# Loads in order of need, two pairs of row tiles ahead of the first gradient, and low priority for a table set-up, in a combined forward and backward kernel

## The chip, the cores and the metric

The kernel runs on one core of a Trainium2 chip. The metric is the device time of one execution in microseconds (us); where a kernel ran several times, the median is given. Engines: PE is the tensor engine, VectorE is DVE in the profile's lines, ScalarE is ACT, GpSimd is POOL, SyncE (SP, its queue SPq) issues the loads. A "tile" of rows below is 128 of the 2048 rows. `L123` in a line of the profile is a line of that kernel's source, so numbers differ by a few between kernels.

## The reference, cut to what matters

```python
def _B_ref(x, W_gate, W_up, W_down):                 # the MLP branch
    gate = einsum("bsd,df->bsf", x, W_gate)
    up = einsum("bsd,df->bsf", x, W_up)
    h = gate * (gate > 0) * up
    return einsum("bsf,fd->bsd", h, W_down)

x = A_q                                              # [1, 2048, 1024] bf16, F = 3584
xn = _layernorm(x)
out = x + _A_ref(xn, ...) + _B_ref(xn, W_gate, W_up, W_down)   # _A_ref: long convolution with 4 shift taps
# wanted: out and the gradients of all inputs for a given grad_out
```

Nearly everything is matrix products of 128 x 128 by 128 x 512. The convolution branch needs tables of sines and the shift taps in transposed form; its steps are woven between the products of the MLP.

## The kernel before: the parts that the change touches

The kernel is written against a scheduler. It lists each engine's instructions in one fixed order, by priority (`pri.now()` is high and grows weaker down the program, `pri.late()` is weaker than all of those) among what its own model of time holds to be ready. On the chip each engine then follows that list.

```python
# the start of the program
b.ln_load(x, a.frm, "frm", 0)                        # rows of tile 0
first = b.weights(B_W_gate, B_W_up, B_W_down, 0)     # W_down by transposing loads
b.layer_norm(x, xn_d, a.frm, "frm", a.tmp, "tmp", a.sm)   # loads tiles 1-3, 4-7, 8-11, 12-15; norm of all
with tc.issue_after(b.ln_act.ins), tc.issue_after(b.ln_dve.ins):
    a.tables()                                       # pri.now(); ends with the taps:
    #   load sk_b; transpose on PE; copy; store
...
# one chunk of the norm, n tiles
for j in range(n): nc.scalar.activation(..., func=ACT.Copy, accum_out=...)      # ScalarE reads the tile: sum
...                                                                              # VectorE: mean
for j in range(n):
    V.tensor_scalar(out=xt[:, j, :], ..., op0=ALU.subtract)                      # VectorE
    nc.scalar.activation(..., func=ACT.Square, accum_out=...)                    # ScalarE
...                                                                              # 3 small VectorE operations
nc.scalar.activation(out=f(4), in_=f(3), func=ACT.Sqrt)                          # ScalarE
...                                                                              # 8 small VectorE operations
for j in range(n): V.tensor_scalar(..., scalar1=self.rstd[...], op0=ALU.mult)    # VectorE; then stored
...
# hidden(): for each pair of tiles (first half: 4 pairs), with 4 PSUM buffers of 512 columns
#   2 x gate (8 matmuls each) -> relu on ScalarE
#   2 x up   (8 matmuls each) -> 2 operations on VectorE, store of h
#   transposes of the next pair on PE (flip_xn) -> copy xnT on VectorE
#   2 x gradient of h (8 matmuls each) -> copy on ScalarE, product on VectorE, store
```

## Time and profile before

| what | before |
|---|---|
| time | 2040.27 us (2038.81 to 2040.48, 3 runs) |
| span of the profiled execution | 2037.0 us |
| PE busy | 1930.9 us, 95% |
| VectorE, ScalarE busy | 995.2 us (49%), 690.4 us (34%) |
| PE idle in the first 100 us | 42 us |

PE is the engine that bounds the kernel, so only time in which it waits can be won. The prediction shows the lines that say so. When reading them, keep one caution in mind: in this profile PE has 10806 matmul records against 11014 weight loads, so 208 records are missing, and idle times of about 0.2 us scattered over the span can be such gaps and no waits.

### The profile page before, as it was taken

The page shows a single profiled execution, that of the slowest core. Times are in us where ns is not written, and L with a number is a line of the kernel's source. Part 1 is how long each engine was busy: PE and PEld are TensorE (multiplying, and loading weights), DVE is VectorE, ACT ScalarE, POOL GpSimd, SP SyncE. Part 2 cuts the span into 40 slices and gives each one's busy share as a digit, 9 for nine tenths or more (in the row PEclk, how much of TensorE's full clock was granted, in tenths as well). Part 3 has the DMA queues.
Part 4 walks back from the last instruction along what each step waited for, and adds up shares of the span by engine and source line. Part 5 has one row for each costly group of instructions (what it writes and reads, how often), then busy time and mean ns, then how long its engine had stood idle before and what let it go on. Part 6 is the DMA issues. An engine that isn't in the chain of part 4 may idle for free. (4 is left out here: it accounts for less than half of the span.)

```text
span 2037.0 us, 27072 instructions
## 1 busy us (share of the span) xinstructions
PE 1930.9 (95%) x10806; PEld 914.7 (45%) x11014; DVE 995.2 (49%) x1444; ACT 690.4 (34%) x902; POOL 20.1 (1%) x46
## 2 busy tenths in 40 slices
PE   4799999999999989999899999999989999999998
PEld 2345445444444445444444544444434444444443
DVE  4848578677687677565575740000112222223332
ACT  6456366356356347474655731111000000000000
POOL 1000000000000000000000000000000000000000
PEclk9899999999999999999999999999999999999999
DMA  9764666865565674545535269332899554454551
GB/s 266 203 160 125 160 159 172 196 174 169 156 167 161 167 192 135 152 131 153 179 119 162 73 169 334 106 119 83 182 257 233 150 134 114 114 126 119 122 128 45
DMA packets 616095, 319.10 MB, mean 157 GB/s; under 512 B 450080, under 2 KB 585248, under 8 KB 615968
## 3 DMA queue, kind: packets, MB, share of 16 engines
q1 hardware_dynamic: 614688, 313.16, 58.5%
q0 software_dynamic: 1280, 4.20, 0.6%
q8 instruction: 86, 1.41, 0.3%
q14 instruction: 41, 0.34, 0.1%
HBM read 141.36 MB, written 95.44 MB: 116 GB/s over the span
## 5 line engine op out<-in xcount | busy, mean ns | idle before, releaser
L673 PE MATMUL ps_w<-ugs,xn_nat 128*128 128x512 bf16 x1746 | 395.3, 380 | 2.7 <-issue 0.5
L673 PEld LDWEIGHTS <-xn_nat 128*128 128x128 bf16 x1792 | 171.5, 98 | 202.9 <-issue 7.1
L576 PEld LDWEIGHTS <-xnT 128*128 128x128 bf16 x1792 | 169.3, 98 | 201.2 <-issue 18.7
L576 PE MATMUL ps_h<-wdT,goT 128*128 128x512 bf16 x865 | 205.7, 382 | 13.4 <-DVE ru L634 11.4
L576 PE MATMUL ps_g<-wg,xnT 128*128 128x512 bf16 x875 | 207.8, 383 | 4.2 <-DVE ru L634 2.6
L576 PE MATMUL ps_u<-wu,xnT 128*128 128x512 bf16 x870 | 205.6, 380 | 1.7 <-issue 0.5
L673 PE MATMUL ps_d<-g_nat,hs 128*128 128x512 bf16 x866 | 203.1, 380 | 4.1 <-DMA ug_d<-ru 1.4
L757 PE MATMUL ps_o<-wd,hT 128*128 128x512 bf16 x878 | 195.0, 382 | 9.8 <-DMA hT<-h_d 8.9
L790 PE MATMUL ps_x<-wgT,ggT 128*128 128x512 bf16 x878 | 197.5, 379 | 1.0
L790 PE MATMUL ps_x<-wuT,guT 128*128 128x512 bf16 x878 | 197.3, 379 | 0.9
L759 DVE TENSOR_TENSOR o<-ps_o,ya 128x512 bf16<-128x512 f32 x32 | 21.5, 687 | 270.4 <-PE ps_o L757 269.8
L711 ACT CAST wi<-ps_w 128x512 bf16<-128x512 f32 x112 | 65.4, 585 | 255.8 <-PE ps_w L673 245.0
L757 PEld LDWEIGHTS <-hT 128*128 128x128 bf16 x896 | 87.7, 98 | 116.9 <-DMA hT<-h_d 10.8
L790 PEld LDWEIGHTS <-ggT 128*128 128x128 bf16 x896 | 87.6, 98 | 105.7
L790 PEld LDWEIGHTS <-guT 128*128 128x128 bf16 x896 | 87.6, 98 | 105.7
L576 PEld LDWEIGHTS <-goT 128*128 128x128 bf16 x896 | 84.9, 98 | 111.7 <-issue 20.2
L646 ACT CAST gh<-ps_h 128x512 bf16<-128x512 f32 x112 | 65.5, 586 | 202.5 <-PE ps_h L576 120.4
L792 DVE CUSTOM_DVE_ANT_0 gx<-ps_x,gy 128x512 f32<-128x512 f32 x32 | 22.1, 691 | 226.6 <-PE ps_x L790 212.5
L673 PEld LDWEIGHTS <-hs 128*128 128x128 bf16 x896 | 82.6, 98 | 98.7 <-issue 9.1
L281 DVE STREAM_TRANSPOSE flp<-B 128x1024 f32<-128x1024 f32 x48 | 90.1, 1934 | 47.8 <-ACT B L69 47.8
L634 DVE SCALAR_TENSOR_TENSOR ru<-ru,ps_u 128x512 bf16<-128x512 bf16 x112 | 76.0, 680 | 73.8 <-PE ps_u L576 47.9
L69 ACT CAST B<-ps 128x1024 bf16<-128x1024 f32 x96 | 95.6, 1020 | 36.0 <-PE ps L65 35.8
(152 smaller groups left out, 1707.9 us busy)
## 6 DMA issues: line engine op xcount, KB each, us to landing
ug_d<-ru SPq DMA_DIRECT2D x112, 256.0 KB, 3.4
ugs<-ug_d SPq DMA_DIRECT2D x112, 256.0 KB, 4.7
wg<-in_B_W_gate_dram SPq DMA_DIRECT2D x56, 256.0 KB, 3.4
wu<-in_B_W_up_dram SPq DMA_DIRECT2D x56, 256.0 KB, 4.6
h_d<-ht SPq DMA_DIRECT2D x112, 128.0 KB, 1.7
hs<-h_d SPq DMA_DIRECT2D x56, 256.0 KB, 4.4
out_dram<-wi SPq DMA_DIRECT2D x56, 256.0 KB, 2.1
gt<-in_grad_out_dram SPq DMA_DIRECT2D x32, 256.0 KB, 3.8
```

The costliest lines, as they stand in the source:

```text
L69: self.nc.scalar.copy(out=out, in_=in_)
L281: self.nc.vector.transpose(out=df[:, c0:c0 + 32, :], in_=sf[:, c0:c0 + 32, :])
L576: self.nc.tensor.matmul(ps[:], lhsT=xT[:, kt * P:(kt + 1) * P], rhs=w(kt), start=(kt == 0), stop=(kt == self.DT - 1))
L634: nc.vector.scalar_tensor_tensor(out=ru[s][:, 1, :], in0=ru[s][:, 0, :], scalar=0.0, in1=ps[:], op0=ALU.is_gt, op1=ALU.mult)
L646: nc.scalar.copy(out=gh[:], in_=ps[:])
L673: self.nc.tensor.matmul(ps[:], lhsT=lhsT(st), rhs=rhs(st), start=(st == 0), stop=(st == self.ST - 1))
L711: nc.scalar.copy(out=wo[:, d, :], in_=ps[:])
L757: nc.tensor.matmul(ps[:], lhsT=hT[:, kt, :], rhs=self.wd[:, kt, oc], start=(kt == 0), stop=(kt == self.FT - 1))
L759: nc.vector.tensor_tensor(out=o0[:, oc], in0=ps[:], in1=ya[:, oc], op=ALU.add)
L790: nc.tensor.matmul(ps[:], lhsT=T[:, kt, :], rhs=W[:, kt, oc], start=(i == 0), stop=(i == n - 1))
L792: V.tensor_tensor_reduce(out=gx[:, oc], in0=ps[:], in1=gy[:, oc], scale=1.0, scalar=0.0, op0=ALU.add, op1=ALU.add, accum_out=m[:, ob:ob + 1])
```

## The change

The intent is to shorten the start: bring the rows in the order in which PE needs them, give PE work that needs neither W_down nor the gradient while those load, take the wait for the taps' load off PE, load the table of the square root before it is needed, and keep the sine tables from blocking VectorE. The diff, cut to its core:

```diff
 def tables(self):
-    pri.now()
+    pri.late()
 ...
-    (taps: load, transpose on PE, copy on VectorE, store)
+def load_shift(self): ...            # the load alone
+def shift_rows(self): ...            # transpose, copy on ScalarE, store: now at the start of the convolution's steps
 ...
+    one = self.per.tile([P, 1], F32, name="one")
+    self.nc.vector.memset(one[:], 1.0)
+    self.nc.scalar.activation(out=one[:], in_=one[:], func=ACT.Sqrt)
 ...
-    LN_CHUNKS = (1, 3, 4, 4, 4)
+    LN_CHUNKS = (1, 1, 2, 4, 4, 4)
 ...  hidden():
+                ahead = fb + half == 0
+                if ahead:
+                    yield from gate_up(0)
                 for sp in range(0, HS, 2):
 ...                 (loads of the gradient's tiles)
+                    if ahead:
+                        if sp + 2 < HS:
+                            yield from gate_up(sp + 2)
+                    else:
+                        yield from gate_up(sp)
+                    yield from grad(sp)
 ...  main:
-    b.ln_load(x, a.frm, "frm", 0)
-    first = b.weights(B_W_gate, B_W_up, B_W_down, 0)
+    load(0)                                               # tile 0
+    first = [b.col_block(B_W_gate, 0, "wg")]
+    load(1)                                               # tile 1
+    first.append(b.col_block(B_W_up, 0, "wu"))
+    load(2)                                               # tiles 2, 3
+    load(3)                                               # tiles 4 to 7
+    first.append(b.row_block_T(B_W_down, 0, "wdT"))
+    goT = [b.load_T(g, i, "goT") for i in range(4)]
+    load(4)                                               # tiles 8 to 11
+    a.load_shift()
+    load(5)                                               # tiles 12 to 15
```

More of the change, by code (lines that the diff above doesn't have):

```diff
@@ L200, in tables, with load_shift, shift_rows @@
             V.tensor_copy(out=self.ident32[b:b + 32, 0, :], in_=self.identA[b:b + 32, b:b + 32])
-        sk_b = con.tile([P, self.NG * 4], BF16, name="sk_b")
-        nc.sync.dma_start(out=sk_b[:].rearrange("c (g i) -> c g i", i=4),
-                          in_=self.shift_k.rearrange("(g c) i -> c g i", c=P))
-        ps = self.ps.tile([self.NG * 4, P], BF16, name="ps_sk", tag="aps")
-        nc.tensor.transpose(ps[:], sk_b[:], self.identA[:])
-        sk_t = con.tile([self.NG * 4, P], BF16, name="sk_t")
-        V.tensor_copy(out=sk_t[:], in_=ps[:])
-        nc.sync.dma_start(out=self.sk_d, in_=sk_t[:])
+    def load_shift(self):
+        self.sk_b = self.con.tile([P, self.NG * 4], BF16, name="sk_b")
+        self.nc.sync.dma_start(out=self.sk_b[:].rearrange("c (g i) -> c g i", i=4),
+                               in_=self.shift_k.rearrange("(g c) i -> c g i", c=P))
+    def shift_rows(self):
+        ps = self.ps.tile([self.NG * 4, P], BF16, name="ps_sk", tag="aps")
+        self.pri.now()
+        self.tc.keep_in_program_order(self.nc.tensor.transpose(ps[:], self.sk_b[:], self.identA[:]))
+        sk_t = self.con.tile([self.NG * 4, P], BF16, name="sk_t")
+        self.act(sk_t[:], ps[:])
+        self.store(self.sk_d, sk_t[:])
     def tview(self, ap2d, cg):
@@ L374, in steps @@
     def steps(self):
+        self.shift_rows()
         nx = self.loads_1(0)
@@ L518, in ln_load, with layer_norm @@
         self.ln_x.append(xt)
-    def layer_norm(self, x, xn_d, xpool, xtag, jpool, jtag, spool):
+    def layer_norm(self, xn_d, jpool, jtag, spool):
         nc, D, V = self.nc, self.D, self.nc.vector
@@ L523, in layer_norm @@
         st0 = 0
-        for i in range(1, 5):
-            self.ln_load(x, xpool, xtag, i)
         for i, n in enumerate(self.LN_CHUNKS):
@@ L603, in flip_xn, with hidden @@
         return xT
-    def hidden(self, first, Wg, Wu, Wd, g, xn_d, h_d, ug_d):
+    def hidden(self, first, goT, Wg, Wu, Wd, g, xn_d, h_d, ug_d):
         nc, HS = self.nc, self.ST // 2
@@ L611, in hidden @@
             xT = [self.load_T(xn_d, s0 + i, "xnT") for i in range(HS)] if half else []
-            if not half:
-                xT += [self.flip_xn(0), self.flip_xn(1)]
-            gT = []
+            gT = [] if half else goT
             for fb in range(self.FB):
@@ L618, in hidden, with gate_up @@
                 wg, wu, wd = first if fb + half == 0 else self.weights(Wg, Wu, Wd, fb)
-                for sp in range(0, HS, 2):
-                    self.pri.now()
-                    if len(gT) < HS:
-                        gT += [self.load_T(g, s0 + sp + s, "goT") for s in range(2)]
-                    ru = [self.e2_tile("ru") for _ in range(2)]
-                    for s in range(2):
+                ru = {}
+                def gate_up(sp):
+                    while len(xT) < sp + 2:
+                        xT.append(self.flip_xn(len(xT)))
+                    for s in (sp, sp + 1):
+                        ru[s] = self.e2_tile("ru")
                         ps = self.ps_tile("ps_g")
-                        self.gemm8(ps, xT[sp + s], wg)
+                        self.gemm8(ps, xT[s], wg)
                         nc.scalar.activation(out=ru[s][:, 0, :], in_=ps[:], func=ACT.Relu)
@@ L629, in hidden @@
                         self.pri.now()
-                    for s in range(2):
+                    for s in (sp, sp + 1):
                         ps = self.ps_tile("ps_u")
-                        self.gemm8(ps, xT[sp + s], wu)
+                        self.gemm8(ps, xT[s], wu)
                         ht = self.e1_tile("ht")
@@ L636, in hidden, with grad @@
                         nc.vector.tensor_tensor(out=ht[:], in0=ru[s][:, 0, :], in1=ru[s][:, 1, :], op=ALU.mult)
-                        nc.sync.dma_start(out=h_d[(s0 + sp + s) * P:(s0 + sp + s + 1) * P, cols], in_=ht[:])
+                        nc.sync.dma_start(out=h_d[(s0 + s) * P:(s0 + s + 1) * P, cols], in_=ht[:])
                         yield 1730
                         self.pri.now()
-                    if len(xT) < HS:
-                        xT += [self.flip_xn(len(xT) + s) for s in range(2)]
-                    for s in range(2):
+                def grad(sp):
+                    for s in (sp, sp + 1):
                         ps = self.ps_tile("ps_h")
-                        self.gemm8(ps, gT[sp + s], wd)
+                        self.gemm8(ps, gT[s], wd)
                         gh = self.e1_tile("gh")
@@ L648, in hidden @@
                             "p (o f) -> p o f", o=1).to_broadcast([P, 2, 512]), op=ALU.mult)
-                        nc.sync.dma_start(out=ug_d[(s0 + sp + s) * P:(s0 + sp + s + 1) * P, :, cols], in_=ru[s][:])
+                        nc.sync.dma_start(out=ug_d[(s0 + s) * P:(s0 + s + 1) * P, :, cols], in_=ru[s][:])
                         yield 1730
                         self.pri.now()
+                ahead = fb + half == 0
+                if ahead:
+                    yield from gate_up(0)
+                for sp in range(0, HS, 2):
+                    self.pri.now()
+                    while len(gT) < min(sp + 2, HS):
+                        gT.append(self.load_T(g, s0 + len(gT), "goT"))
+                    if ahead:
[4 more added lines that the diff above has]
+                    yield from grad(sp)
     def slab(self, src, fb, name):
@@ L862 @@
     pri.now()
-    b.ln_load(x, a.frm, "frm", 0)
-    first = b.weights(B_W_gate, B_W_up, B_W_down, 0)
-    b.layer_norm(x, xn_d, a.frm, "frm", a.tmp, "tmp", a.sm)
+    load = lambda i: b.ln_load(x, a.frm, "frm", i)
+    load(0)
[9 more added lines that the diff above has]
+    load(5)
+    b.layer_norm(xn_d, a.tmp, "tmp", a.sm)
     with tc.issue_after(b.ln_act.ins), tc.issue_after(b.ln_dve.ins):
@@ L869, in mlp @@
     def mlp():
-        yield 0.9, b.hidden(first, B_W_gate, B_W_up, B_W_down, g, xn_d, h_d, ug_d)
+        yield 0.9, b.hidden(first, goT, B_W_gate, B_W_up, B_W_down, g, xn_d, h_d, ug_d)
         yield 1.3, b.grad_down(g, h_d, out_9)
@@ L874 @@
     a_steps, left = a.steps(), A_START
-    for pace, phase in mlp():
-        for ns in phase:
-            left -= ns * pace
-            while a_steps is not None and left <= 0:
-                d = next(a_steps, None)
-                if d is None:
-                    a.close()
-                    a_steps = None
-                    b.open_right(B_W_down)
-                else:
-                    left += d
+    if True:
+        for pace, phase in mlp():
+            for ns in phase:
+                left -= ns * pace
+                while a_steps is not None and left <= 0:
+                    d = next(a_steps, None)
+                    if d is None:
+                        a.close()
+                        a_steps = None
+                        b.open_right(B_W_down)
+                    else:
+                        left += d
     b.close_left()
```

## The prediction

> **What bounds the kernel now.** I read the span in slices first, then busy time in stretches of 50 us, then the tensor engine's waits in the first 120 us, then the order of time there.
>
> The page's part 2, busy tenths and granted clock in 40 slices of 51 us:
>
> ```profile
> PE   4799999999999989999899999999989999999998
> ...
> PEclk9899999999999999999999999999999999999999
> ```
>
> PE is the bound (1930.9 of 2037.0 us busy), and only the first two slices are clearly low. Three stretches put a size on it; the first figure after the stretch's length is PE's busy time:
>
> ```profile
> 0.00:50.00 50.00, 20.75 (x126) 11.05 (x128) 22.53 (x83) 33.31 (x63) 9.12 (x23) 1.00 1.01 269
> 50.00:100.00 50.00, 37.16 (x185) 17.36 (x187) 45.40 (x105) 22.84 (x34) 4.79 (x9) 0.90 0.77 196
> 100.00:150.00 50.00, 49.74 (x252) 22.06 (x256) 23.46 (x33) 25.98 (x34) 0.00 (x0) 1.00 0.63 165
> ```
>
> PE is idle for 29.2 + 12.8 = 42 us of the first 100, and for 0.3 us of the next 50. The other 64 us of idle time lie later (scattered waits up to 1250 us, 9 us around 1500 us, the last stores), where the diff changes nothing. In the same first 50 us the DMA share is 1.01: the queues are full, so a load's place in the queue is its time. PE's waits in that stretch (total, times, longest):
>
> ```profile
> PE ps_sk L205 <- DMA sk_b<-in_A_shift_k_dram: 16.1, 1, 16.1
> PE pst_x L600 <- DVE ln_x L558: 12.2, 2, 10.3
> PE ps_h L576 <- DVE ru L634: 11.4, 2, 10.5
> PE pst_x L600 <- ACT ru L627: 1.8, 1, 1.8
> ```
>
> They make 41.5 of the 42 us. In order of time on PE, with the idle time before each piece in brackets:
>
> ```profile
> 10.35 1.03 PE L600 MATMUL pst_x<-ident,ln_x 128*128 128x128 bf16 x8 [10.35 <-DVE ln_x L558]
> 27.47 0.29 PE L205 MATMUL ps_sk<-identA,sk_b 128*32 128x128 bf16 x1 [16.09 <-DMA sk_b<-in_A_shift_k_dram]
> 29.58 1.04 PE L600 MATMUL pst_x<-ident,ln_x 128*128 128x128 bf16 x8 [1.82 <-DVE ln_x L558]
> 30.41 5.95 PE L576 MATMUL ps_g<-wg,xnT 128*128 128x512 bf16 x16
> ```
>
> and on the queue that issues the loads:
>
> ```profile
> 5.24 7.37 SPq L584 DMA_TRANSPOSE wdT<-in_B_W_down_dram  x4
> 12.65 2.32 SPq L517 DMA_DIRECT2D ln_x<-in_A_q_dram  x4
> 15.02 2.88 SPq L202 DMA_DIRECT2D sk_b<-in_A_shift_k_dram  x1
> ```
>
> The tap transpose stands on PE ahead of the second row tile's transpose and waits for a tiny load that was issued behind everything. But taking it away alone gives little: the second tile is ready only at 29.2 us, because rows 128 to 511 are loaded after all the weights of W_down (ScalarE starts on them at 18.78 us). The 10.5 us hole at 68.7 us is another thing: VectorE works through the sine tables from 62.5 to 77.6 us, and only then through what PE waits for:
>
> ```profile
> 77.87 0.69 DVE L647 TENSOR_TENSOR ru<-ru,gh 128x1024 bf16<-128x1024 bf16 x1
> 78.48 1.28 DVE L634 SCALAR_TENSOR_TENSOR ru<-ru,ps_u 128x512 bf16<-128x512 bf16 x2
> ```
>
> **What the Trainium skill says.** (1) "TensorE: Matmul & The Clock Gate", Part 2, step by step: matmuls stay in program order, only weight loads are pulled ahead. The trace agrees: one 0.29 us transpose held PE for 16.1 us. Its "Architectural detail" says that ScalarE and VectorE are strict FIFO; the hole at 68.7 us agrees. (2) The same page, "What's actually happening": after an idle window of about 3.4 us the clock falls to half. Agrees: the first 16 big matmuls take 5.95 us against 3.62 later, and after the hole 14 take 4.62. (3) "DMA: Bandwidth & Descriptors", "Issuing engines are not separate DMA queues": all share the same 16 engines. Agrees with the share of 1.01. (4) "ScalarE: Activation LUTs", "What ACT_TABLE_LOAD costs": about 1283 ns plus a drain. The trace shows 1.28 us in the first tile's chain, at 6.72 us; whether a drain adds to it the view doesn't show (the activation follows at once).
>
> **The change part by part.**
> *Sqrt activated at the start*: the table load leaves the first tile's chain. First transpose at 10.35 - 1.28 = 9.1 us. Gain 1.3 us, on the path.
> *Order of loads*: rows of tile 1 right after the gate weights, tiles 2 and 3 after the up weights, tiles 4 to 7 next, then W_down, the gradient's four tiles, the rest. No bytes are added. Bytes in front decide. Before, 4.2 MB of loads (and a 0.26 MB store) were in front of the end of tiles 1 to 3 and the data was there at 18.78 us; the first 0.26 MB was there at 3.48 us: 0.27 MB/us over a stretch with slow transposing loads, 0.3 to 0.37 without them (295 to 364 GB/s at 2 to 8 us). At 0.33: tile 1 (1.57 MB) at 7.5 us, tiles 2 and 3 (3.15 MB) at 12 to 13, tiles 4 to 7 (4.2 MB) at 16, W_down (5.2 MB) at 20, the gradient (6.3 MB, with stores of normalized rows) at 25 to 27.
> *Norm after landing*: the one-tile chunk took 10.35 - 3.48 - 1.28 = 5.6 us from landing to PE, so tile 1 is ready at 13.5. The three-tile chunk took 29.58 - 18.78 = 10.8; one tile fewer is about 1.04 x 2 on ScalarE and 0.5 on VectorE less, so 8.2: tiles 2 and 3 at about 21. Tiles 4 to 7 took 38.3 - 26.2 = some 14 to 15 us when chunks follow each other; ScalarE is then in line behind tiles 2 and 3 and four evictions of 0.59, so they come at 33 to 34.
> *PE's work in that order*: to 21 us it has two transposes of 1.03, four groups of 8 matmuls at 1.73, and the cold clock's 2.3: 11.3 us. Idle to 21 us: about 10. Then two transposes, gate and up of tiles 2 and 3 (9.0) and the first gradient pair (3.5) last to 33.5, when tiles 4 and 5 are due: 0 to 2 us more. That is what running ahead buys: 9 us of work that needs neither W_down nor the gradient.
> *Taps*: transposed some 35 groups later, when its load is long there: the 16.1 us wait goes (it overlapped the wait for tile 1).
> *Tables late*: VectorE takes them when nothing else is ready. One op is at most 2.6 us against four PSUM buffers of 1.73 us each, so of 10.5 us I leave 1.5.
> *Sum*: head idle before 42. After: 10 + 1 + 1.5, plus 1 for late taps and 3 for waits in the crowded part (before it had 0.9 + 1.8 there, and stores now queue behind the transposing loads): 16.5. Gain 25.5, and about 1 us of slow clock after the hole: 26.5. All of it is on PE, the bound, so it should reach the end: 2040.3 - 26.3 = **2014**.
>
> **Rivals.** (a) *Stores and their three buffers become the wait.* The products h and the copied gradients share three buffers that come free when a store has landed; with two pairs ahead, the fourth product needs the first store's end, and that store is issued behind W_down and the gradient (issue time 1.9 us each, eight of them, to about 22 us). For: ScalarE already waits 8.4 us in two pieces for such stores. Against: PE lost none of it. It would leave 5 to 10 us more: 2020 to 2024. (b) *VectorE is the bound up to 100 us.* From 15 to 90 us it has roughly 25 us of norm, 24 of the MLP, 18 of tables, 12 of the convolution's first products and 5 of copies, 84 us in 75. For: it was busy 45 of 50 us. Against: only a small part of it is needed by PE at once; convolution work that comes late is hidden unless PE's order has it early. Tap rows come later too, so the shifted keys start 10 us or more nearer to their use. It would cost 5 to 12: 2019 to 2026. (c) *The norm is paced by ScalarE, so earlier loads only move the wait.* It has 33 us of norm anyway. I count on tiles 0 to 7 alone being needed early; if the order on ScalarE were worse than that, 2022. (d) *Everything goes well*: idle of 10 us and better luck later, 2006.
>
> **Range and chances.** The centre is 2014. One rival in part costs 5 to 10, the scattered waits from 250 to 1250 us (some 45 us in all) can shift by 5 either way when the schedule is built anew. Range 2004 to 2027. Faster by over 2% means below 1999.5, nearly the whole head idle gone: 0.03. Slower by 2% means 2081, for which nothing speaks: 0.01.
>
> **What would show it.** Right: no wait of the tap transpose; first big matmul before 16 us; PE busy about 84 of the first 100 us (58 before); no hole near 70 us; the clock row at full in the second slice. Rival (a) shows as PE or VectorE waiting for the landing of h stores at 20 to 45 us; (b) as PE waits for flips or products between 80 and 150 us; (c) as PE waiting on the normalized rows at 15 to 40 us. I'd be wrong if PE's idle time after 100 us grew by 10 us or more.

## The result, and the profile after

The changed kernel takes 2030.03 us (median of 4 runs, 2027.46 to 2031.13) against 2040.38 of the same rounds. Ratios in this document are the mean time of one kernel's fast runs over that of the other's fast runs of the same rounds, so not quite the ratio of the medians: here 0.9949, with a 95% interval of 0.9932 to 0.9966. That is a gain of 10 us where 26 were forecast, and outside the range of 2004 to 2027.

In the slices of the page, the second is full now (9 tenths of PE instead of 7), but the first is as empty as before (4). Busy time in stretches of 50 us, PE first:

```profile
0.00:50.00 50.00, 22.22 (x97) 10.56 (x98) 27.87 (x105) 37.02 (x72) 11.51 (x26) 0.90 1.07 287
50.00:100.00 50.00, 47.82 (x245) 22.46 (x244) 37.54 (x95) 21.46 (x30) 2.41 (x5) 1.00 0.85 207
```

PE is idle for 27.8 + 2.2 = 30 us of the first 100, where it was 42 before and 16.5 were forecast. The fall of 12 us answers to the span's fall of 11.3 (2037.0 to 2025.7), so in this pair of profiles the gain of the head did reach the end; it was only smaller. (One pair is no proof: a second profile of the changed kernel, after_again, has 33.1 us of idle time there and a span of 2023.7.) PE's waits in the first 120 us:

```profile
PE ps_g L584 <- DVE xnT L610: 11.3, 4, 6.8
PE pst_x L608 <- DMA wu<-in_B_W_up_dram: 9.6, 1, 9.6
PE pst_x L608 <- ACT ru L634: 4.6, 1, 4.6
PE pst_x L608 <- DVE ln_x L566: 4.4, 1, 4.4
```

The wait for the taps and the hole behind the tables are gone by name. What took their place is new: transposed rows (xnT), and a PSUM buffer that a gate's eviction (ru) holds. (The 9.6 us are the start; the load named there is the last that came, the order of time shows VectorE's norm of tile 0 ending at 9.57.) In order of time on PE, with the idle time before each piece in brackets:

```profile
9.62 1.03 PE L608 MATMUL pst_x<-ident,ln_x 128*128 128x128 bf16 x8 [9.62 <-DMA wu<-in_B_W_up_dram]
15.02 1.03 PE L608 MATMUL pst_x<-ident,ln_x 128*128 128x128 bf16 x8 [4.36 <-DVE ln_x L566]
22.89 6.05 PE L584 MATMUL ps_g<-wg,xnT 128*128 128x512 bf16 x16 [6.84 <-DVE xnT L610]
28.77 3.62 PE L584 MATMUL ps_u<-wu,xnT 128*128 128x512 bf16 x16
37.03 1.87 PE L608 MATMUL pst_x<-ident,ln_x 128*128 128x128 bf16 x16 [4.64 <-ACT ru L634]
41.22 5.42 PE L584 MATMUL ps_g<-wg,xnT 128*128 128x512 bf16 x16 [2.32 <-DVE xnT L610]
```

Both transposes are done at 16.05 us, and yet the first gate starts at 22.89. VectorE shows why:

```profile
15.83 0.88 DVE L547 TENSOR_SCALAR ln_x<-ln_x,ln_s 128x1024 bf16<-128x1024 bf16 x2
18.63 0.17 DVE L551 TENSOR_SCALAR ln_b<-ln_s 128x2 bf16<-128x2 f32 x1 [1.92 <-ACT ln_j L550]
...
21.35 0.88 DVE L566 TENSOR_SCALAR ln_x<-ln_x,rstd 128x1024 bf16<-128x1024 bf16 x2
22.15 1.28 DVE L610 COPY xnT<-pst_x 128x1024 bf16<-128x1024 bf16 x2
```

The two copies that PE needs stand in VectorE's list behind the whole norm of tiles 2 and 3. VectorE even idles in between (1.92 us before the second line), but it takes its list in order. The second hole is the same on ScalarE:

```profile
32.13 1.06 ACT L543 ACTIVATE ln_j<-ln_x 128x1024 bf16<-128x1024 bf16 x1 [3.54 <-DMA ln_x<-in_A_q_dram]
33.10 0.19 ACT L543 ACTIVATION_READ_ACCUMULATOR ln_j<-ln_x 128x1 f32 x1
33.19 0.19 ACT L554 ACTIVATE ln_s<-ln_s 128x4 f32<-128x4 f32 x1
...
36.40 1.06 ACT L634 ACTIVATE ru<-ps_g 128x512 bf16<-128x512 f32 x2
```

The first line is the first reading of tile 8. Nothing needs it so early: the first load that reads back normalized rows of all tiles, for the convolution, is issued at 66.37 us, and the MLP's second half loads them from 336.69. It waits until 32.13 us for its load. Behind it stand the square root of tiles 4 to 7 (33.19), three more readings of 1.04 us (tiles 9 to 11) and then the evictions of the first two gates (36.40), whose products were done by about 28.8. The load is that late because of where it now stands in the queue:

```profile
8.02 11.18 SPq L592 DMA_TRANSPOSE wdT<-in_B_W_down_dram  x4
19.24 6.17 SPq L601 DMA_TRANSPOSE goT<-in_grad_out_dram  x4
25.46 0.58 SPq L527 DMA_DIRECT2D ln_x<-in_A_q_dram  x1
```

Eight transposing loads hold the issuing queue for 17 us, and the rows of tile 8 are issued behind them.

### The profile page after: what moved, and what is told of

Same layout as the page of the kernel before. It is cut to its first block, busy times and chain, and to the rows that moved or that the text cites. A ratio compares the mean times of both kernels' runs of the same rounds, so it can differ in the third digit from the quotient of the medians.

```text
span 2025.7 us, 27299 instructions
## 1 busy us (share of the span) xinstructions
PE 1948.7 (96%) x11014; PEld 916.3 (45%) x11014; DVE 996.8 (49%) x1457; ACT 690.8 (34%) x904; POOL 20.1 (1%) x46
## 5 line engine op out<-in xcount | busy, mean ns | idle before, releaser
L694 PE MATMUL ps_w<-ugs,xn_nat 128*128 128x512 bf16 x1792 | 399.8, 380 | 0.0
L584 PE MATMUL ps_g<-wg,xnT 128*128 128x512 bf16 x896 | 212.3, 386 | 14.0 <-DVE xnT L610 11.3
L694 PE MATMUL ps_d<-g_nat,hs 128*128 128x512 bf16 x896 | 209.5, 382 | 1.3 <-DMA hs<-h_d 1.2
L584 PE MATMUL ps_u<-wu,xnT 128*128 128x512 bf16 x896 | 210.3, 381 | 0.0
L694 PEld LDWEIGHTS <-hs 128*128 128x128 bf16 x896 | 83.1, 98 | 99.4 <-issue 11.3
```

Source lines behind the costliest of these rows:

```text
L584: self.nc.tensor.matmul(ps[:], lhsT=xT[:, kt * P:(kt + 1) * P], rhs=w(kt), start=(kt == 0), stop=(kt == self.DT - 1))
L694: self.nc.tensor.matmul(ps[:], lhsT=lhsT(st), rhs=rhs(st), start=(st == 0), stop=(st == self.ST - 1))
```

## The experiments

My theory after reading this: the head is set by the order in which ScalarE and VectorE hold their work. The norm of tiles that are not yet needed stands ahead of the copies and evictions that PE waits for; the late load of tile 8 makes it worse. The main rival: the norm itself is too slow, so that a better order only moves the wait. A second: a gain in the head is lost later. All kernels below gave correct results. "Head idle" is the sum of PE's bracketed idle times in the first 100 us of the profiled run.

| kernel | median us | before, same rounds | ratio (95% interval) | head idle, us |
|---|---|---|---|---|
| changed kernel | 2030.03 | 2040.38 | 0.9949 (0.9932, 0.9966) | 30.0 |
| e1 rows early | 2025.93 | 2040.12 | 0.9925 (0.9906, 0.9943) | 30.9 |
| e2 norm from tile 8 late | 2020.84 | 2040.12 | 0.9899 (0.9884, 0.9914) | 26.7 |
| e3 first copies ahead | 2032.24 | 2040.12 | 0.9954 (0.9929, 0.9978) | 33.8 |
| e4 = e2 + e3 | 2023.47 | 2040.12 | 0.9902 (0.9878, 0.9925) | 25.2 |
| u1 tables at old priority | 2039.79 | 2044.10 | 0.9981 (0.9966, 0.9996) | 38.3 |
| u2 no running ahead | 2028.62 | 2044.10 | 0.9928 (0.9913, 0.9942) | 29.7 |
| u3 old order of loads | 2032.31 | 2044.10 | 0.9946 (0.9929, 0.9962) | 34.9 |
| f2 = e3 + norm from tile 4 late | 2027.28 | 2044.10 | 0.9920 (0.9906, 0.9935) | 27.8 |
| b1 before + taps moved | 2038.08 | 2036.56 | 1.0006 (0.9983, 1.0029) | 44.2 |
| g1 = f2 + tile 8 behind a square root | 2018.95 | 2036.56 | 0.9915 (0.9889, 0.9940) | 24.3 |
| g5 = g1 without running ahead | 2022.11 | 2036.56 | 0.9923 (0.9901, 0.9946) | 26.2 |
| g7 norm from tile 2 late | 2022.16 | 2036.56 | 0.9934 (0.9909, 0.9959) | 29.4 |
| changed kernel, again | 2026.28 | 2038.20 | 0.9939 (0.9919, 0.9959) | 33.1 |
| e2 again | 2020.77 | 2038.20 | 0.9913 (0.9897, 0.9929) | 27.1 |
| g1 again | 2019.40 | 2038.20 | 0.9908 (0.9891, 0.9924) | 25.0 |
| g8 = g1 + first gate early | 2017.30 | 2038.20 | 0.9895 (0.9877, 0.9913) | 25.1 |

The kernel before has 2036.6 to 2044.1 us in the four sets, so times are compared by ratio, and closely only within a set (a set is a block of rows with the same time of before).

### First set: which order costs what

**e1**, rows of tiles 8 to 15 ahead of W_down:

```diff
     load(3)
+    load(4)
+    load(5)
     first.append(b.row_block_T(B_W_down, 0, "wdT"))
     goT = [b.load_T(g, i, "goT") for i in range(4)]
-    load(4)
     a.load_shift()
-    load(5)
```

> Edit: the rows of tiles 8 to 15 are loaded right behind those of tiles 4 to 7, ahead of W_down and the gradient. Theory (order on ScalarE and VectorE): in the changed kernel ScalarE's first reading of tile 8 waits until 32.1 us for its load, and the square root of tiles 4 to 7 and the first two gate evictions stand behind it (36.4 us), so PE idles 4.6 + 2.3 us. Here that wait goes and the evictions run by 31 us; the built order puts the first two transposed copies even further back on VectorE (behind the subtraction for tiles 4 to 7, 25 us instead of 22.2), so only part shows: 2026 to 2029 us against 2030. Rival (norm too slow anyway, or gains lost after 100 us): 2030. Second rival (W_down and gradient are needed as early as they come now): 2032 or more.

Measured 2025.93, ratio 0.9925. The wait for a PSUM buffer at 32 us is gone and the gates' evictions run at 32.13 instead of 36.40, but the first gate starts at 25.46 (9.43 us of idle time in front of it), as the built order had said. W_down and the gradient, now later, cost nothing: the first gradient product runs at 45.08 us with no idle time before it. The time is at the lower end of the theory's range, but the interval overlaps the changed kernel's, and the head idle of this profiled run (30.9) doesn't show a gain either; this profile has the 208 missing records again, and its own run was the slowest of the four.

**e2**, the norm of tiles 8 to 15 at low priority, loads untouched:

```diff
             xt = self.ln_x[i]
-            self.pri.now()
+            step = self.pri.late if i >= 4 else self.pri.now
+            step()
```

(and the same `step()` ahead of the last scaling).

> Edit: the norm of tiles 8 to 15 gets the low priority, so the MLP's evictions go ahead of it; loads as in the changed kernel. Theory: relus of the first two gates at 29 to 30 us instead of 36.4, the second pair's gates at 35 to 36 instead of 41.2: PE idle in the first 100 us from 30 to 25, time about 2025. Rival (norm too slow): the second pair's gates still start at 40 us or later, 2030. Rival (late norm delays the convolution branch or the second half): slower than 2032.

Measured 2020.84, better than expected. ScalarE in e2:

```profile
28.41 1.05 ACT L635 ACTIVATE ru<-ps_g 128x512 bf16<-128x512 f32 x2
29.37 0.20 ACT L555 ACTIVATE ln_s<-ln_s 128x4 f32<-128x4 f32 x1
32.98 1.06 ACT L544 ACTIVATE ln_j<-ln_x 128x1024 bf16<-128x1024 bf16 x1 [3.42 <-DMA ln_x<-in_A_q_dram]
```

Tile 8 still waits for its load until 33 us, but the evictions and the square root are ahead of it now, 8.0 and 3.8 us earlier than in the changed kernel. The second pair's gates start at 35.09 instead of 41.22, against the rival's 40 or later. So the late load alone did PE no harm here; what stood behind it did. (The edit moved VectorE's part of that norm back as well, so it doesn't tell the two lists apart.) The convolution lost little by the late norm: its first load of normalized rows moved from 66.37 to 79.37 us, but the VectorE product behind it only from 87.6 to 88.1.

**e3**, the copies of tiles 0 and 1 right behind the subtraction for tiles 2 and 3 on VectorE:

```diff
+            if i == 2:
+                self.xT0 = [self.flip_xn(0), self.flip_xn(1)]
+                es.enter_context(self.tc.issue_after(self.flip_copy.ins))
             V.tensor_scalar(out=b(1), ...)
```

> Edit: the transposed copies of tiles 0 and 1 go on VectorE right behind the subtraction for tiles 2 and 3, ahead of the rest of that norm. Theory: the first gate starts at about 18 us instead of 22.9, but all four PSUM buffers are full after two gates and two ups and the relus still stand behind the reading of tile 8 (32.1 us): PE goes on at 36 to 37 us as before, and nothing is gained: 2028 to 2031. Rival (each hole is worth its own length): 2025.

Measured 2032.24, ratio 0.9954: nothing gained. On PE:

```profile
17.68 4.92 PE L589 MATMUL ps_g<-wg,xnT 128*128 128x512 bf16 x16 [1.32 <-DVE xnT L615]
22.44 3.62 PE L589 MATMUL ps_u<-wu,xnT 128*128 128x512 bf16 x16
38.78 1.86 PE L613 MATMUL pst_x<-ident,ln_x 128*128 128x128 bf16 x16 [12.73 <-DVE ln_s L546]
```

The first gate starts 5.2 us earlier, and the next hole is 12.7 us long instead of 4.6, because the relus run at 38.16 (1.8 us later than in the changed kernel, since tile 8 was read at 33.89 instead of 32.13). The hole of 6.84 us was not worth its length: PE had filled its four PSUM buffers and stood until a relu emptied one. A wait that is removed ahead of a later one that doesn't move is only shifted.

**e4**, both.

> Edit: e2 and e3 together. Theory: first gate at 18 us, relus at 27 to 29, second pair's gates at 33 to 34 instead of 41.2: PE idle in the first 100 us about 21 to 22 instead of 30, time 2020 to 2022; the two together gain more than the sum of the two alone. Rival (norm too slow): not under 2027. Rival (gains are lost later): PE idle falls in the head and the time stays above 2026.

Measured 2023.47, ratio 0.9902, the same as e2 (0.9899) and a little above what I expected. That the two together would gain more than their sum did not come true. The first gate is at 17.38 us, but the second pair's gates are at 35.01 as in e2: the copies of tiles 2 and 3 (VectorE at 33.87) again stood behind the norm of the next chunk, tiles 4 to 7.

### Second set: parts of the change undone, and one repair

**u1**: `pri.late()` in `tables` back to `pri.now()`.

> Edit: in the changed kernel the tables get the old priority back, all else stays. Theory (the prediction's term for the tables): the built order again puts all 40-odd table operations on VectorE ahead of the MLP's, so PE has a hole of about 10 us near 65 to 80 us and the slow clock after it: 2039 to 2042 against 2030. Rival: with the pairs run ahead and PE late anyway the hole is short: 2030 to 2033.

Measured ratio 0.9981, 4.3 us under before and some 6 to 9 us over the changed kernel (ratio 0.9949, or 0.9939 in the last set). The hole is back:

```profile
74.93 1.87 PE L608 MATMUL pst_x<-ident,ln_x 128*128 128x128 bf16 x16 [8.81 <-DVE ru L641]
```

The time lies in the expected 2039 to 2042, but this set's before is 4 us slower than that figure assumed; by ratio the tables' low priority is worth 6 to 9 us, not 10.

**u2**: `ahead = False`.

> Edit: in the changed kernel gate and up of a pair of tiles are again followed by that pair's gradient; all else stays. Theory: W_down and the gradient's tiles have landed before PE could use them (the first gradient product ran at 49.9 us with no wait), and PE is held by evictions and copies: running ahead gains nothing, 2027 to 2031. Rival (the prediction's step: it buys up to 9 us of work while W_down is on its way): 2035 to 2039.

Measured ratio 0.9928. Running ahead shows no gain here, the gates' evictions hold PE in this order just the same (4.83 us at 37 us).

**u3**: all weights, then all rows, taps, gradient.

> Edit: in the changed kernel the loads go in the old order (all three weights, then all rows, taps, gradient); the rest stays. Theory: tile 1 comes at about 18 us as in the kernel before and the first gate starts at 27 to 29 us instead of 22.9, but ScalarE no longer waits for tile 8: part of it comes back, 2031 to 2036. Rival (order of loads is the main gain): 2040.

Measured ratio 0.9946, the same as the changed kernel's 0.9949. Tile 1 is late again:

```profile
23.22 1.03 PE L608 MATMUL pst_x<-ident,ln_x 128*128 128x128 bf16 x8 [12.51 <-DVE ln_x L566]
```

but the first gate (30.14 us) then meets a ScalarE that isn't waiting for tile 8, and the wait for a PSUM buffer is 0.69 us. So the new order of loads gains 7.2 us at the first gate and gives about half of it back at the evictions: the second pair's gates start at 45.05 instead of 41.22, and the next block of weights at 87.65 instead of 81.87 (83.75 in the changed kernel's second profile). The 4 to 6 us that the profiles keep don't show in the ratios, but those come from different rounds, and with intervals of 0.0017 to either side a difference of 4 or 5 us could hide in them. The worth of the new order alone stays open between nothing and about 5 us.

**f2**: e4, with the low priority from tile 4 on (`i >= 3`).

> Edit: as e4, but the low priority of the norm starts with tile 4 instead of tile 8. In e4 the copies of tiles 2 and 3 stood on VectorE behind the norm of tiles 4 to 7 (PE idle 5.3 us at 30 us), now the built order has them ahead. Theory: second pair's gates at 30 to 31 us instead of 35.0, PE idle in the first 100 us about 18 to 20, time 2017 to 2019. Rival (then the norm of tiles 4 to 7 comes too late): a hole of 4 us or more moves to 40 to 50 us, time 2021 to 2024 as e2 and e4.

Measured ratio 0.9920: no better than e4 (the intervals overlap), and the hole moved, though not for the reason that the rival gave. ScalarE and PE in f2:

```profile
32.74 1.06 ACT L545 ACTIVATE ln_j<-ln_x 128x1024 bf16<-128x1024 bf16 x1 [4.02 <-DMA ln_x<-in_A_q_dram]
33.80 0.19 ACT L559 ACTIVATE ln_s<-ln_s 128x4 f32<-128x4 f32 x1
```

```profile
37.03 6.00 PE L590 MATMUL ps_g<-wg,xnT 128*128 128x512 bf16 x15 [7.66 <-DVE ht L649]
```

With both chunks at low priority the scheduler again put the first reading of tile 8 ahead of the square root of tiles 4 to 7. VectorE's list had that norm's next operation in the midst of the evictions, so it stood still from 29.4 to 34.0 us and PE with it.

### Third set: the order pinned, and the taps

**b1**: the kernel before with only the taps' transpose moved (the diff's `load_shift` and `shift_rows`).

> Edit: the kernel before, with only the transpose of the shift taps moved to the start of the convolution's steps. Theory (the prediction's claim that this alone gives little): the 16.1 us wait of PE for the taps' load disappears by name, but PE then waits for the rows of tile 1 until 29.2 to 29.6 us all the same, and the hole at 68.7 us stays: ratio to before 0.998 to 1.001. Rival (the wait was worth its length): ratio 0.992.

Measured ratio 1.0006. The wait of 16.1 us is gone and the one for tile 1 is longer by as much:

```profile
29.95 1.03 PE L607 MATMUL pst_x<-ident,ln_x 128*128 128x128 bf16 x8 [18.70 <-DVE ln_x L565]
```

**g1**: f2, and the norm of tile 8 and on pinned behind that square root.

```diff
             es = ExitStack()
+            if i == 4:
+                es.enter_context(self.tc.issue_after(self.ln_act.ins))
```

> Edit: f2 with one more constraint: ScalarE's and VectorE's norm of tile 8 and on is placed behind the square root of tiles 4 to 7. In f2 ScalarE's first reading of tile 8 again got ahead of that square root and waited for its load to 32.7 us; VectorE stood behind it with the evictions and copies, and PE idled 7.7 us. Theory: that hole goes, second pair's gates at 31 us instead of 37.0, ratio to before 0.987 to 0.989 (2015 to 2017 where before has 2040). Rival (the load itself or the norm's length is the bound): ratio 0.991 as f2.

Measured 2018.95, ratio 0.9915 (0.9889 to 0.9940). The profile does what was expected in kind: the second pair's gates start at 32.93 instead of 37.03, with 3.30 us of idle time in front instead of 7.66, and the head idle is 24.3. In time it missed the expected 0.987 to 0.989, and the interval is too wide to tell it from f2.

**g5**: g1 without running ahead.

> Edit: g1 without running ahead, the first pair's gradient follows its own gate and up. Theory: W_down and the first gradient tiles land by 27 to 31 us, when PE would take them in this order at 27: a wait of 0 to 4 us, but tiles 2 and 3 are then needed later; within 3 us of g1, so running ahead is worth little even without the holes. Rival (it buys up to 9 us): 6 to 9 us over g1.

Measured ratio 0.9923, within 3.2 us of g1 by the medians, with overlapping intervals. The four runs of each (2015.70 to 2024.97 and 2017.64 to 2023.73) have means 1.8 us apart; they speak against a loss of 9 us, and are too scattered to exclude one of 6. (A gradient's copy waits here for a store of h, 4.78 us until 41.7 us, the wait of the prediction's rival (a). PE's hole of 6.43 us is over before that: it ends with a VectorE copy at 38.57.)

**g7**: the changed kernel with low priority from tile 2 on, tile 8 pinned as in g1.

> Edit: the changed kernel with low priority for the norm from tile 2 on, and that of tile 8 and on behind the square root of tiles 4 to 7; no explicit place for the first copies. Theory: first gate at 22 to 23 us as in the changed kernel, then no long hole, second pair's gates at 31 to 33: ratio 0.989 to 0.991, a little behind g1. Rival (late norm of tiles 2 and 3 delays them): second pair's gates at 35 or later, ratio 0.992.

Measured ratio 0.9934, above both the theory's and the rival's figure. The second pair is at 32.95 us as expected, but the third pair's gates wait 4.82 us at 49.75. Low priority alone hands the wait on to the next chunk.

### Fourth set: one chip, five rounds

**The changed kernel, e2 and g1 again.**

> The changed kernel itself, as the measure for the three beside it on one chip. Both theories: ratio to before 0.993 to 0.997.

> e2 again (norm of tiles 8 to 15 at low priority). Theory that the evictions behind the reading of tile 8 are the larger part of what was missing: ratio 0.989 to 0.991, so 7 to 11 us under the changed kernel.

> g1 again (first copies ahead, norm from tile 4 at low priority, tile 8 behind the square root of tiles 4 to 7). Theory: its head idle (24 us by the profile) is 2 to 3 us under that of e2 (26.6), so ratio 0.988 to 0.990. Rival: the first hole is worth nothing even now, ratio equal to that of e2 or above.

Measured 0.9939, 0.9913 and 0.9908. e2 is 5.5 us faster than the changed kernel by the medians (2026.28 and 2020.77), a bit less than expected. The ratios' intervals just overlap, but five of the changed kernel's six runs are slower than every run of e2 (2019.81 to 2022.75). The head idle is 6.0 us less (33.1 and 27.1), so this gain was not lost later. g1 is 1.4 us faster than e2, with overlapping intervals: with the evictions ahead, the first hole is still not shown to be worth anything in time, and my expectation of 0.988 to 0.990 was missed. The changed kernel's own second hole was 7.5 us long in this profiled run against 4.6 in the first, so it varies from run to run with the landing of tile 8.

**g8**: g1, with the first tile's gate on PE ahead of the second tile's transposes, and the norm of tiles 2 and 3 behind that of tile 1.

```diff
+            if i == 1:
+                self.xT0 = [self.flip_xn(0)]
+                es.enter_context(self.tc.issue_after(self.flip_copy.ins))
             if i == 2:
-                self.xT0 = [self.flip_xn(0), self.flip_xn(1)]
+                self.ru0, ps = self.e2_tile("ru"), self.ps_tile("ps_g")
+                self.gemm8(ps, self.xT0[0], wg)
+                nc.scalar.activation(out=self.ru0[:, 0, :], in_=ps[:], func=ACT.Relu)
+                with self.tc.issue_after(self.mm_last.ins):
+                    self.xT0.append(self.flip_xn(1))
                 es.enter_context(self.tc.issue_after(self.flip_copy.ins))
```

> Edit: g1, with the first tile's gate on PE ahead of the second tile's transposes (its copy on VectorE right after tile 1's subtraction) and the norm of tiles 2 and 3 behind that of tile 1. Tests the prediction's figure of 10 us of PE idle up to 21 us, which silently let PE use the wait for tile 1. Theory: first gate at 11.5 to 12 us instead of 17.3, PE idle up to 22 us 11 to 12 us instead of 15.3; if no new hole opens in front of tiles 4 to 7, ratio 0.986 to 0.988. Rival: the norm of tiles 4 to 7 comes later in this order (its subtraction stands behind the copies of tiles 2 and 3) and a hole of 3 to 5 us at 38 to 42 us takes the gain: ratio as g1.

Measured 2017.30, ratio 0.9895. On PE:

```profile
11.43 3.36 PE L602 MATMUL ps_g<-wg,xnT 128*128 128x512 bf16 x8 [0.79 <-DVE xnT L628]
...
16.82 1.90 PE L602 MATMUL ps_g<-wg,xnT 128*128 128x512 bf16 x8 [1.52 <-DVE xnT L628]
...
44.11 1.89 PE L626 MATMUL pst_x<-ident,ln_x 128*128 128x128 bf16 x16 [9.09 <-DVE ln_x L583]
```

Up to 22 us PE is idle for 9.61 + 0.79 + 1.52 = 11.9 us, where the changed kernel has 20.8 up to 22.9. Then a hole opens, longer than the 3 to 5 us of the rival and not for its reason. The norm of tiles 4 to 7 is late, but VectorE shows that it waited for something else:

```profile
32.60 0.17 DVE L572 RECIPROCAL ln_s<-ln_s 128x4 f32<-128x4 f32 x1
41.82 0.42 DVE L666 TENSOR_TENSOR ht<-ru 128x512 bf16<-128x512 bf16 x1 [9.04 <-DMA h_d<-ht]
...
43.56 0.88 DVE L583 TENSOR_SCALAR ln_x<-ln_x,rstd 128x1024 bf16<-128x1024 bf16 x2
```

VectorE was already behind the square root of that norm (first line). Next in its list stood the fourth product h, which needs one of three buffers, and these come free when a store of h has landed. The first product was written at 23.2 us; the first three stores were issued at 34.39, 36.78 and 38.39 us, behind the loads on the same queue. ScalarE waited 7.49 us for such a store too. This is the wait that the prediction had described as its rival (a).

g8 is still 9.0 us under the changed kernel and 20.9 under before by the medians, the best kernel by the median; against g1 and e2 the intervals overlap, though four of its five runs are below every run of e2. If this hole went too there would be at most about 9 us more to win (an estimate from the 9.09 us in front of 44.11, not tried).

## Why the prediction was wrong, point by point

**What held.** PE's head idle decides, and in the profiles of the result the gain came out at the end almost undiminished (12.0 us of idle time, 11.3 of span). The taps alone were worth nothing (b1), and no wait for them appeared later. The tables' hole went, and came back when their priority was restored (u1), at 6 to 9 us by ratio (9 in the sum). Landing times were near: tiles 2 and 3 were read from 13.13 us (12 to 13 forecast) and normalized at 22.2 (21 forecast); W_down and the gradient were never waited for. Of the signs that it named, the waits for the taps and at 70 us did go; the first big product before 16 us (22.89) and PE busy for 84 of the first 100 us (70.0) did not come.

**The step that failed** is "Idle to 21 us: about 10" with the one behind it, "when tiles 4 and 5 are due: 0 to 2 us more". The data was there and PE was free, but the sum left out the lists of the two engines between them. Up to the first gate PE idled 20.8 us instead of 10, after it 7.0 instead of 1, and later 2.2 where the sum had allowed 5.5: 13.5 us more in all. Three pieces make it up:
- It let PE work while tile 1 was normalized. In the built order both transposes are ahead of the first gate, as `gate_up` in the diff writes them, so PE idled 4.4 us there. g8, built the way the sum had assumed, has 11.9 us of idle time up to 22 us, close to the figure. But in that order rival (a) then costs 9.1 us, which the sum didn't hold: it would not have come true even so.
- It gave VectorE's copies no place. They stood behind the norm of tiles 2 and 3, 6.8 us. e3 showed that this hole is not additive: removed alone it gained nothing, and e4 and g1, which removed the later one too, don't show a worth for it either.
- It took ScalarE's order as tiles 0 to 7 first. In fact the first reading of tile 8 came ahead of the square root of tiles 4 to 7 and of the evictions, and waited for a load that the change itself had moved behind 17 us of transposing loads: 4.6 us. (The 2.3 us behind it end with a VectorE copy and stayed in e2, at 2.9.) This is the piece whose repair alone shows in time (e2: 5.5 us on one chip, 9 in the first set against the result's rounds). Such an order was there to be read in the kernel before: its first reading of tiles 4 to 7, at 26.16 us, stands ahead of the square root of tiles 1 to 3 at 27.20, and the next chunk's at 36.48 ahead of 37.52. There the rows had landed, and it cost about 1 us each time. The prediction had named it as rival (c), "if the order on ScalarE were worse than that, 2022", and then gave it little weight.

**Sizes that were off.** The table load was said to give 1.3 us; it gave 0.73 (10.35 to 9.62), since three small VectorE operations had run beside it and now stand alone in the chain. The slow clock was said to cost 1 us less; the first gates took 6.05 and the second pair's 5.42 us against 3.62 when warm, 4.2 us lost, where before lost 2.3 at the first gates and about 1.8 after the hole (16 products from 79.21 to 84.47 us, 3.45 when warm). So it cost no less; the transposes at 37.03 (1.87 us against 1.06) add 0.8. "That is what running ahead buys: 9 us" was wrong as a gain: u2 and g5 show none that can be told from zero. The order of loads, which the sum had as the largest gain, shows none in time in this built order (u3), since half of what it wins at the first gate it loses at the evictions.

**Slips in the working** that changed little: "38.3 - 26.2" is 12.1, but the trace has that norm from 26.16 to 41.04 us, so the 14 to 15 stand. The sum's gain is 26.5 and 26.3 was taken off. The 64 us of idle time after the head counted some 14 us of missing records as waits. And a DMA share of 1.01 shows busy DMA engines; it is no test of what the cited page says about issuing from several engines.

**What stays open.** By the sum, 13.5 us more idle time than forecast leaves about 2.5 us of the 16 between 2014 and 2030; 1 to 2 are the clock, and the rest is within the spread of the changed kernel's runs (2027.46 to 2031.13, and 2021.66 to 2029.90 on another chip). Why the scheduler's model places tile 8's reading so early was not examined; only that its order doesn't match the landing times of the chip was seen. And of the three pieces only the last has a worth in time that a run shows; the first two are read from the trace.

## What to carry to other kernels

Before you add up the waits that a change removes, write down for each engine that stands between a load and the bound engine the order in which it will take its work; an instruction for data that comes late blocks everything behind it, however urgent (3.5 to 5.5 us on ScalarE here, by the landing of tile 8). Count buffers that wait for a store in the same way: their stores may stand behind the loads that you moved forward. When loads are reordered, the consumers of those that moved back must move back too: low priority for the norm of the rows that are needed last gained as much as half of the original change again. And when two waits follow each other, removing the earlier one alone may show nothing.

## What the Trainium skill lacked or had wrong

- "DMA: Bandwidth & Descriptors", "Issuing engines are not separate DMA queues" calls the sequencer's time to start a transfer "usually small relative to the DMA itself". Here four transposing loads held the issuing queue for 11.18 us and four more for 6.17, while the plain loads issued before them took about 0.5 us each; the loads behind them were late for that. It is no fixed cost of a transposing load: the same four took 7.37 us in the kernel before, and four plain loads behind them, at 17.95 us, took 8.34.
- "ScalarE: Activation LUTs", "What ACT_TABLE_LOAD costs" adds a drain of about 1380 ns to the load of about 1283 ns. In the kernel before the load takes 1.28 us from 6.72 and the activation follows at 8.02, so no drain shows there; and removing it from the chain gave 0.73 us, since other work had run beside it.
- "TensorE: Matmul & The Clock Gate", "What's actually happening" gives half the clock after an idle window, and g8's first 8 gate matmuls agree (3.36 us, against 1.90 for 8 later). This is no lack of the page, but the granted clock of the profile doesn't show it: in the kernel before it read 1.00 from 30 to 40 us, while 16 matmuls took 5.95 us instead of 3.62.
- No page says that matmul records can be missing from a profile: 10806 against 11014 weight loads in the kernel before, none missing in the profile after. Small idle times on PE need not be waits then.
